# Splitting two weight loads by partition rows, and widening the row sums, in a grouped-query attention kernel

## The chip, the cores and the metric

The kernel runs on one core of a Trainium2 chip. The metric is device time in microseconds (us) of one execution; times quoted are medians. A ratio is the mean time of one kernel's fast runs over the mean of the other's fast runs in the same rounds on the same chip, so it is not quite the ratio of the quoted medians. "Fast" excludes runs more than 1.5% above the fastest of the same kernel.

## The reference

```python
# B=8, Sq=4, D=512, Hq=32, Hkv=8, Sk=2048, Dh=128, all bf16
q = (x @ wq).reshape(B, Sq, Hq, Dh).transpose(0, 2, 1, 3)
k = jnp.repeat(k_cache, 4, axis=1); v = jnp.repeat(v_cache, 4, axis=1)
scores = jnp.einsum("bhqd,bhkd->bhqk", q, k) * Dh ** -0.5
p = softmax(scores)
o = jnp.einsum("bhqk,bhkd->bhqd", p, v)
out = o.transpose(0, 2, 1, 3).reshape(B, Sq, Hq * Dh) @ wo
```

The K and the V cache are 33.6 MB each, wq and wo 4.2 MB each. Everything is read once, 75.5 MB in all, and little is written.

## The kernel before

All loads go out on one queue, from SyncE, in program order: x, wq, then K and V in blocks of 1 MiB (two heads of one batch, a "unit"; there are 32), then wo in blocks of 1 MiB and less. Every load but the small one of x (32 rows) covers 128 partitions. The code is shortened here and below.

```python
def load_wo(p, r0, n):
    rows = wo[p * HP * 128 : (p + 1) * HP * 128, :].rearrange("(q r) j -> q r j", r=WR)
    nc.sync.dma_start(wo_sb[:, p, r0 : r0 + n, :], rows[:, r0 : r0 + n, :])

nc.sync.dma_start(x_sb[:, :], x.flatten_outer_dims())
nc.sync.dma_start(wq_sb[:, :, :], wq.rearrange("(p r) n -> p r n", r=R))   # 128 rows of 32 KB
# ... K and V loads; after the last V load:
for w in range(G2 - 1):
    load_wo(w, 0, WR)            # three blocks: 128 rows of 8 KB
load_wo(G2 - 1, 0, 4); load_wo(G2 - 1, 4, 2); load_wo(G2 - 1, 6, 2)
```

The row sums of the softmax come from products with a matrix of ones, added up by VectorE (DVE):

```python
LC = 8
def norms(u):
    l_ps = psum_l.tile([128, LC, NQ], FP32, tag="l", name="l_ps")     # NQ = 32
    for c in range(0, C, LC):                                          # C = 32
        nc.tensor.matmul(l_ps[:, :, :], lhsT=ones[:, :], rhs=pr[:, c : c + LC, :],
                         start=(c == 0), stop=(c + LC == C))
    nc.vector.tensor_reduce(out=l_sb[:, :], in_=l_ps[:, :, :].rearrange("d c q -> d q c"),
                            axis=AX, op=ADD)
    nc.vector.reciprocal(r_sb[:, :], l_sb[:, :])

for step in range(-L - 1, NH):          # two steps (hf = 0, 1) to a unit
    # ... transposes of K and scores, some steps ahead
    if step >= 0:
        if hf == 1:
            norms(u)
        values(step)
```

The softmax here doesn't subtract the row's maximum and nothing guards it: scores larger than these inputs give would overflow.

Of the kernel before, what the change touches and what calls it, by code (L numbers as in the profile page):

```python
# [7 lines left out]

BF16 = mybir.dt.bfloat16
FP32 = mybir.dt.float32  # L10
EXP = mybir.ActivationFunctionType.Exp


@with_exitstack
def kernel(
# [9 lines left out]
    nc = tc.nc  # L25
# [7 lines left out]
    R = D // 128  # L33
# [12 lines left out]
    WR = HP  # L46
    DH = D // 2
    AX = mybir.AxisListType.X
    LC = 8
    ADD = mybir.AluOpType.add  # L50
    assert Dh == 128 and C == 32 and NQ == 32

# [14 lines left out]
    wq_sb = const.tile([128, R, HqDh], BF16, name="wq_sb")  # L67
# [3 lines left out]
    wo_sb = const.tile([128, G2, WR, D], BF16, name="wo_sb")  # L71
# [29 lines left out]

    def load_wo(p, r0, n):
        rows = wo[p * HP * 128 : (p + 1) * HP * 128, :].rearrange("(q r) j -> q r j", r=WR)
        nc.sync.dma_start(wo_sb[:, p, r0 : r0 + n, :], rows[:, r0 : r0 + n, :])

    nc.sync.dma_start(x_sb[:, :], x.flatten_outer_dims())
    nc.sync.dma_start(wq_sb[:, :, :], wq.rearrange("(p r) n -> p r n", r=R))
    loads = []
    for u in range(NU + KA):
        if u < NU:  # L110
# [27 lines left out]
    for p in range(G2):  # L138
        psq = psum_s.tile([128, HP, T], FP32, tag="s", name="psq")
        for h in range(HP):  # L140
# [30 lines left out]
    def scores(i):  # L171
        u, hf = divmod(i, 2)
        p, b = units[u]
        pr = probs[u % len(probs)]
        s_ps = psum_s.tile([128, HC, NQ], FP32, tag="s", name="s_ps")
        q2 = qT_all[:, p, b, :, :].rearrange("d h s -> d (h s)")
# [5 lines left out]
        for g in range(2):  # L182
            rows = slice(g * 64, (g + 1) * 64)
            cols = slice(g * NQ // 2, (g + 1) * NQ // 2)
            nc.scalar.activation(  # L185
                out=pr[rows, hf * HC : (hf + 1) * HC, cols], in_=s_ps[rows, :, cols], func=EXP
            )
# [3 lines left out]
    def values(i):  # L191
# [3 lines left out]
        if hf == 0:  # L195
            o_ps[u] = psum_o.tile([128, NQ], FP32, tag="o", name="o_ps")
        for c in range(HC):
# [11 lines left out]
    def norms(u):  # L209
        pr = probs[u % len(probs)]  # L210
        l_ps = psum_l.tile([128, LC, NQ], FP32, tag="l", name="l_ps")
        for c in range(0, C, LC):
            nc.tensor.matmul(  # L213
                l_ps[:, :, :],
                lhsT=ones[:, :],
                rhs=pr[:, c : c + LC, :],
                start=(c == 0),
                stop=(c + LC == C),
            )
        l_sb = small.tile([128, NQ], FP32, tag="l_sb", name="l_sb")  # L220
        nc.vector.tensor_reduce(  # L221
            out=l_sb[:, :], in_=l_ps[:, :, :].rearrange("d c q -> d q c"), axis=AX, op=ADD
        )
        r_sb = small.tile([128, NQ], FP32, tag="r_sb", name="r_sb")
        nc.vector.reciprocal(r_sb[:, :], l_sb[:, :])  # L225
# [38 lines left out]
    for step in range(-L - 1, NH):  # L264
        i, j = step + L + 1, step + L
        if i < NH:
            transpose_part(i, 0)
        if 0 <= j < NH:
            scores(j)
        if i < NH:  # L270
            transpose_part(i, 1)
        u, hf = divmod(step, 2)
        if step >= 0:
            p, b = units[u]
# [4 lines that stand above are left out]
                finish(u)  # L279
            elif p > 0 and b == 1:  # L280
                to_tokens(p - 1)
            elif p > 0 and b == 2:
                to_wo_rows(p - 1)
        load_ready(min((i + 1) // 2, NU), max((step + 1) // 2, 0))
        if step == NH - 1 - 2 * VB:
            assert not loads
            for w in range(G2 - 1):
                load_wo(w, 0, WR)
            load_wo(G2 - 1, 0, 4)
            load_wo(G2 - 1, 4, 2)  # L290
            load_wo(G2 - 1, 6, 2)
# [54 lines left out]
```

## Time and profile before

| | before |
|---|---|
| time, median (lowest to highest) | 195.31 us (194.30 to 196.41) |
| span in the profile | 193.6 us |
| mean rate of the loads | 393 GB/s |
| last V load lands | 178.23 us |
| last wo load lands | 188.17 us |
| last matrix product ends | 190.38 us |

The next line is from the page of the kernel before, the part in 40 equal slices of the span (4.84 us each): how much the DMA engines moved in each slice.

```profile
GB/s 223 433 386 423 421 423 415 425 418 413 420 415 420 416 420 418 421 416 418 418 420 418 418 420 423 416 416 416 416 421 416 421 420 418 415 420 418 321 107 7
```

Apart from the first slice and the last three, the rate is about 420 GB/s. Such a flat line suggests that the transfers set the pace and not an engine; the chain in the prediction agrees, most of it being waits for loads. The prediction below shows how the end of the kernel is read.

### The profile page before, as it was taken

The numbers are of one execution on the slowest core, as the hardware profiler recorded it, in microseconds if no ns is written. First come the engines' busy times: TensorE is split into PE (matmuls) and PEld (weight loads), VectorE is DVE, ScalarE is ACT, GpSimd is POOL, SyncE is SP. The second block draws the span as 40 slices with busy tenths as digits, with TensorE's granted clock in tenths as the row PEclk, the third lists the DMA queues.
The fourth block names the chain that finished last, engine by engine and source line by source line (L and its number), as shares of the span: only waits on it lengthen the run. The fifth ranks groups of instructions, "written<-read, shape, count | busy, mean of one in ns | idle before, by whom it ended". The sixth has DMA issues, their size and how long they took to land.

```text
span 193.6 us, 7489 instructions
## 1 busy us (share of the span) xinstructions
PE 147.5 (76%) x3428; PEld 135.4 (70%) x3428; DVE 99.0 (51%) x211; ACT 84.0 (43%) x166; POOL 0.7 (0%) x6
## 2 busy tenths in 40 slices
PE   1029768999888786977777799878787799785893
PEld 0029768888788776877777788777777788774441
DVE  6003454666656554655555576555555576544300
ACT  2003766555555554444555555424455555550000
POOL 1000000000000000000000000000000000000000
PEclk9999999999999999999999999999999999999699
DMA  6999999999999999999999999999999999999720
GB/s 223 433 386 423 421 423 415 425 418 413 420 415 420 416 420 418 421 416 418 418 420 418 418 420 423 416 416 416 416 421 416 421 420 418 415 420 418 321 107 7
DMA packets 10352, 76.05 MB, mean 393 GB/s; under 512 B 1168, under 2 KB 1232, under 8 KB 1616
## 3 DMA queue, kind: packets, MB, share of 16 engines
q1 hardware_dynamic: 10320, 75.57, 94.2%
q8 instruction: 27, 0.44, 0.9%
q14 instruction: 5, 0.04, 0.1%
HBM read 75.53 MB, written 0.03 MB: 390 GB/s over the span
## 4 chain that ended last, share of the span: by engine, by line
DMA 79%; PE 12%; ACT 3%; DVE 2%; issue 1%; SPq 0%; DVEq 0%
DMA k_sb<-in_k_cache_dram 63%; DMA v_sb<-in_v_cache_dram 10%; DMA wq_sb<-in_wq_dram 6%; PE out_ps L297 4%; ACT kt L166 2%; PE kp L163 2%; PE psq L143 2%; DVE kt L168 2%; PE s_ps L179 2%; ACT probs L185 1%; PE o_ps L199 1%; PE l_ps L213 1%; PE nat L242 1%; PE perm L257 0%; DVE l_sb L221 0%
## 5 line engine op out<-in xcount | busy, mean ns | idle before, releaser
L168 DVE COPY kt<-kp 128x1024 bf16<-128x1024 bf16 x96 | 65.6, 688 | 66.9 <-PE kp L163 66.2
L163 PE MATMUL kp<-ident,k_sb 128*128 128x128 bf16 x1024 | 77.0, 219 | 19.7 <-DMA k_sb<-in_k_cache_dram 19.5
L185 ACT ACTIVATE probs<-s_ps 64x256 bf16<-64x256 f32 x128 | 48.4, 378 | 74.1 <-PE s_ps L179 73.4
L163 PEld LDWEIGHTS <-k_sb 128*128 128x128 bf16 x1024 | 58.0, 97 | 23.2 <-DMA k_sb<-in_k_cache_dram 22.0
L179 PE MATMUL s_ps<-qT_all,kt 128*128 128x32 bf16 x1024 | 37.9, 176 | 6.7 <-ACT kt L166 5.1
L179 PEld LDWEIGHTS <-kt 128*128 128x128 bf16 x1024 | 33.1, 96 | 7.5 <-ACT kt L166 6.0
L199 PE MATMUL o_ps<-probs,v_sb 128*128 128x32 bf16 x1024 | 35.7, 176 | 2.7 <-DMA v_sb<-in_v_cache_dram 2.3
L199 PEld LDWEIGHTS <-v_sb 128*128 128x128 bf16 x1024 | 33.4, 96 | 3.9 <-DMA v_sb<-in_v_cache_dram 3.2
L166 ACT COPY kt<-kp 128x1024 bf16<-128x1024 bf16 x32 | 32.4, 1012 | 0.8
L213 PE MATMUL l_ps<-probs,ones 128*128 128x256 bf16 x128 | 19.2, 272 | 0.0
L221 DVE TENSOR_REDUCE l_sb<-l_ps 128x32 f32<-128x256 f32 x32 | 13.3, 416 | 5.2 <-PE l_ps L213 5.2
L225 DVE RECIPROCAL r_sb<-l_sb 128x32 f32<-128x32 f32 x32 | 11.3, 353 | 1.1
L213 PEld LDWEIGHTS <-ones 128*128 128x128 bf16 x128 | 11.0, 98 | 1.0 <-issue 0.2
L143 PE MATMUL psq<-xT_sb,wq_sb 128*128 128x32 bf16 x128 | 3.6, 187 | 9.3 <-DMA wq_sb<-in_wq_dram 9.3
L143 PEld LDWEIGHTS <-wq_sb 128*128 128x128 bf16 x128 | 3.5, 104 | 9.5 <-DMA wq_sb<-in_wq_dram 9.5
L297 PE MATMUL out_ps<-wo_sb,oP 128*32 128x512 bf16 x32 | 8.5, 427 | 0.0
L314 ACT CAST out_sb<-out_ps 32x256 bf16<-32x256 f32 x1 | 0.4, 362 | 17.8 <-DVE out_sb L313 17.8
L230 DVE TENSOR_TENSOR oT_all<-o_ps,r_sb 128x32 bf16<-128x32 f32 x32 | 6.1, 192 | 3.3
L150 ACT ACTIVATE qT_all<-psq 128x256 bf16<-128x256 f32 x4 | 1.5, 385 | 13.8 <-PE psq L143 13.8
L297 PEld LDWEIGHTS <-oP 128*32 128x32 bf16 x32 | 3.4, 109 | 4.3 <-issue 1.7
L248 DVE COPY nat_sb<-nat 32x1024 bf16<-32x1024 bf16 x4 | 2.7, 678 | 3.8 <-PE nat L242 3.8
L262 DVE COPY oP<-perm 128x256 bf16<-128x256 bf16 x4 | 1.2, 292 | 5.1 <-PE perm L257 5.1
(17 smaller groups left out, 16.4 us busy)
## 6 DMA issues: line engine op xcount, KB each, us to landing
k_sb<-in_k_cache_dram SPq DMA_DIRECT2D x32, 1024.0 KB, 19.9
v_sb<-in_v_cache_dram SPq DMA_DIRECT2D x32, 1024.0 KB, 19.9
wq_sb<-in_wq_dram SPq DMA_DIRECT2D x1, 4096.0 KB, 12.2
wo_sb<-in_wo_dram SPq DMA_DIRECT2D x3, 1024.0 KB, 21.3
wo_sb<-in_wo_dram SPq DMA_DIRECT2D x1, 512.0 KB, 20.0
wo_sb<-in_wo_dram SPq DMA_DIRECT2D x2, 256.0 KB, 16.5
x_sb<-in_x_dram SPq DMA_DIRECT2D x1, 32.0 KB, 1.6
out_dram<-out_sb SPq DMA_DIRECT2D x1, 32.0 KB, 1.5
```

The costliest lines, as they stand in the source:

```text
L143: nc.tensor.matmul(psq[:, h, :], lhsT=wq_sb[:, r, hh * 128 : (hh + 1) * 128], rhs=xT_sb[:, r, :], start=(r == 0), stop=(r == R - 1),)
L163: nc.tensor.transpose(kp[:, c, :], ks[u][:, c0 + c, :], ident[:, :])
L166: nc.scalar.copy(out=k_t[:, :, :], in_=kp[:, :, :])
L168: nc.vector.tensor_copy(out=k_t[:, :, :], in_=kp[:, :, :])
L179: nc.tensor.matmul(s_ps[:, c, :], lhsT=k_t[:, c % (HC // 2), :], rhs=q2, start=True, stop=True)
L185: nc.scalar.activation(out=pr[rows, hf * HC : (hf + 1) * HC, cols], in_=s_ps[rows, :, cols], func=EXP)
L199: nc.tensor.matmul(o_ps[u][:, :], lhsT=vs[u][:, cc, :], rhs=pr[:, cc, :], start=(cc == 0), stop=(cc == C - 1),)
L213: nc.tensor.matmul(l_ps[:, :, :], lhsT=ones[:, :], rhs=pr[:, c : c + LC, :], start=(c == 0), stop=(c + LC == C),)
L221: nc.vector.tensor_reduce(out=l_sb[:, :], in_=l_ps[:, :, :].rearrange("d c q -> d q c"), axis=AX, op=ADD)
L225: nc.vector.reciprocal(r_sb[:, :], l_sb[:, :])
L230: nc.vector.tensor_tensor(out=oT_all[:, p * HP : (p + 1) * HP, b, :], in0=o_ps[u][:, :].rearrange("d (h s) -> d h s", h=HP), in1=r_sbs[u][ ...
L297: nc.tensor.matmul(out_ps[:, :], lhsT=oP[p][:, r, :], rhs=wo_sb[:, p, r, :], start=(p == 0 and r == 0), stop=(p == G2 - 1 and r == WR - 1),)
```

## The change

The loads of 128 rows are cut by partition. As the prediction works out, the DMA engines fall into an early and a late group of eight. The change, as the prediction reads it, gives eight engines more rows and the others fewer. The trace doesn't number the engines; "the first eight" are here those that loads of 8 rows use. Moreover each pair of 512-wide products replaces four 256-wide ones, which leaves out 128 PE instructions in all.

```diff
+PARTS = [(0, 112), (112, 120), (120, 128)]
@@
-    LC = 8
+    LC = 16
@@ def load_wo(p, r0, n):
-        nc.sync.dma_start(wo_sb[:, p, r0 : r0 + n, :], rows[:, r0 : r0 + n, :])
+        for lo, hi in PARTS if n == WR else [(0, 128)]:
+            nc.sync.dma_start(wo_sb[lo:hi, p, r0 : r0 + n, :], rows[lo:hi, r0 : r0 + n, :])
@@
-    nc.sync.dma_start(wq_sb[:, :, :], wq.rearrange("(p r) n -> p r n", r=R))
+    for lo, hi in PARTS:
+        nc.sync.dma_start(wq_sb[lo:hi, :, :], wq.rearrange("(p r) n -> p r n", r=R)[lo:hi])
```

## The prediction

The sum of rival B came to 204.3 us. It holds two terms, 7.3 us for the two small wq loads and 5.6 us for the six of wo: they took a packet of an 8-row load to last four times as long (4 x 1.213 = 4.85 us at wq). The factor was assumed. Two milder cases of B came to 200 and 195 us.

> **What bounds the kernel now.** I read the page's utilisation strip first, then the chain of work that ended last (its shares, then in order of time), then the DMA issues, the queue table and the groups. The strip and the queue table:
>
> ```profile
> DMA  6999999999999999999999999999999999999720
> q1 hardware_dynamic: 10320, 75.57, 94.2%
> q8 instruction: 27, 0.44, 0.9%
> ```
>
> The 16 DMA engines are 90% busy or more in slices 2 to 37; 75.57 MB are moved in 193.6 us. Only the last three slices fall off, and not at once (7, 2, 0). That ramp is what the change aims at. The second queue brings instructions: 27 packets, 0.44 MB, so 16 KB each. The chain, in order of time, shows the end:
>
> ```profile
> 1.17 12.16 DMA wq_sb<-in_wq_dram
> ...
> 159.30 18.93 DMA v_sb<-in_v_cache_dram
> 178.23 0.05 issue
> 178.28 0.56 PE o_ps L199 x16
> 178.84 0.46 PE l_ps L213 x4
> 179.30 0.02 issue
> 179.32 0.43 DVE l_sb L221
> ...
> 180.48 1.03 PE nat L242 x8
> 181.52 2.96 PE out_ps L297 x8
> 184.48 0.60 PE perm L257 x8
> 185.09 5.30 PE out_ps L297 x24
> 190.38 0.02 issue
> ```
>
> The end is set by the last V load, landing at 178.23, then 12.15 us of PE and DVE work to 190.38, then 3.2 us of eviction and output store. The last wo load only just stays off this path. A load lands when all 16 increments of its semaphore have come, and the trace holds the time of each. For the last V load they come at 171.63 plus 0.00, 0.13, 0.25, 0.25, 0.29, 0.96, 1.55, 2.44 us, and then 4.68, 4.83, 4.84, 4.93, 4.98, 5.04, 5.12, 6.60 us: **eight DMA engines are early and eight late**, by 0.7 against 5.1 us on average, though all have the same bytes. For the last wo load the eighth comes at 184.04, the ninth at 186.25, the last at 188.17. For the first K load all sixteen lie within 0.41 us, so the gap grows during the run.
>
> Its cause shows in the packet records. The 27 instruction packets start at 19.4, 25.9, 32.4 us and so on, one about every 6.2 us, and take 1.02 to 1.15 us where they meet data. Next to each, one 8 KB data packet takes 0.76 to 0.86 us instead of 0.31, and the lengths recur with every eighth fetch: 0.787 us at 20.4, 70.9, 121.8 and 172.0. So fetches go round eight engines, and each holds one back by about 1.5 us (the largest lag rises 0.41, 1.9, 3.4, 5.1, 6.6 us). Three to four fetches for each of eight engines are the 5 us.
>
> [...]27 packets of 16 KB for 6,858 PE instructions in the build[...]. [...]8 KB packets are almost all 309 to 321 ns long, with no mutual disturbance. [...]in the 32-row x load most 1 KB packets take 44 to 46 ns, but one of 71 and one of 60 overlap, together 85 ns, about two in turn.
>
> **The change part by part.**
> *Rows.* The first eight engines get 9 rows of wq instead of 8, the others 7; the same for three wo blocks. A 32 KB wq packet takes 1.213 us, an 8 KB one 0.31. So the first eight gain 1.21 + 3 x 0.31 = 2.14 us of work, and the last eight lose as much: just half of the 4.4 us gap, clearly the intent. If nothing else happens and the first eight are the early ones, the last V comes at 178.23 - 1.2 = 177.0 (late engines; the early ones, 174.07 + 1.2 = 175.3, are not in the way), and the last wo at about 186.1.
> wq itself is complete 1.2 us later. That delays the compute that catches up from 13.4 to 34.4 us, but queued loads cover it: each landing takes about 20 us from its issue, eight in flight.
> *Row sums.* Four 256-wide matmuls become two 512-wide. Per column PE streams alike: in the chain four take 0.46 us, and 24 matmuls of 512 take 5.30, thus 0.22 each and two 0.44. PE gains nothing on the path.
>
> ```profile
> L221 DVE TENSOR_REDUCE l_sb<-l_ps 128x32 f32<-128x256 f32 x32 | 13.3, 416 | 5.2 <-PE l_ps L213 5.2
> L213 PE MATMUL l_ps<-probs,ones 128*128 128x256 bf16 x128 | 19.2, 272 | 0.0
> L230 DVE TENSOR_TENSOR oT_all<-o_ps,r_sb 128x32 bf16<-128x32 f32 x32 | 6.1, 192 | 3.3
> ```
>
> The reduce reads 512 elements, not 256. Between 32 elements (192 ns, L230) and 256 (416 ns) the slope is 1.0 ns per element, so I estimate 416 + 256 = 672 ns. DVE grows by 32 x 0.256 = 8.2 us to 107, 55% of the span: hidden, except in the tail, where it adds 0.26 us. The builds differ by 128 PE instructions (6,858 to 6,730), half a fetch, worth under 1.5 us on one engine; I count zero.
> Sum if the balance works: -1.2 + 0.26 = **-0.95 us**, 194.3.
>
> **The rivals.**
> A. *The balance works*, as just summed: 194.3. For it: the amounts fit the measured gap exactly. Even then it can't reach 2%: the PE tail of 12.15 us follows V, and only the wq half of the gain comes before V.
> B. *The small loads collide[...].* [...] On the first eight engines the extra is then 2.14 + 7.3 + 5.6 = 15.0 us by the last wo: 184.04 + 15.0 = 199.1, plus two matmuls (0.45) and 3.2 us, plus the 1.6 us by which the measured time exceeds the span: 204.3. If blocks of seven rows collide as well[...], a queue calculation with these durations adds some 4 us: 208.[...] For B: [...]the overlapping pair; against it, most x packets, and that the row counts look chosen by someone who measured.
> C. *The first eight are the late ones.* V lands 1.2 us later, wo at 190.3, and the wo load becomes the end: 190.3 + 0.45 + 3.2 + 1.6 = 195.6; same.[...]
>
> **Range and chances.** I give B in a form that costs over 2% 0.53, and A, C or a mild B 0.45. A leaves a narrow cluster at 194 to 195.6, B a wide one from 199 to 208. The one number is the median of both, **200.0 us**, at B's lower edge; the range is 193.3 to 208.0. Faster by over 2% gets 0.02, since no sum comes near 191.3.
>
> **What would show it.** A: wq packets stay at 1.21 us, the sixteen increments of the last V span 4 us or less, V lands near 177, wo near 186, and the chain is the same with a reduce of about 0.67 us. B: wq packets of the 8-row loads take 3 to 5 us, those of wo up to 1.2, wq lands past 20 us, the DMA strip shows holes near slices 3 to 5, the chain ends in a wo load, and the early group of engines has become the late one. C: the spread at the last V grows to about 9 us. Packets of unchanged length beside a time over 199 would show that I have the wrong cause; so would a DVE or PE group that the chain goes through in the middle.

## The result, and the profile after

The changed kernel takes 219.06 us (218.23 to 221.55) against 195.31: ratio 1.12, 95% interval 1.111 to 1.129. It is slower by some 23 us, and outside the predicted range, on the side of rival B.

From its page: the DMA strip, the rates in its 40 slices (5.44 us each) and the two queues.

```profile
DMA  7999799999999999999999999999999999999730
GB/s 193 247 259 110 84 352 418 420 421 418 417 418 417 414 421 420 420 417 418 418 418 417 423 418 420 415 417 417 423 417 418 420 415 417 242 220 214 226 98 9
q1 hardware_dynamic: 10384, 75.57, 94.3%
q8 instruction: 26, 0.43, 0.8%
```

The two lines must be read together. The strip says that the engines are as busy as ever, 90% or more in nearly all slices. The rates say that while they were "busy" they moved 247 and 259 GB/s in slices 2 and 3, 110 and 84 in slices 4 and 5 (the strip has a 7 for slice 5), and 214 to 242 in slices 35 to 38. Between, in the loads of K and V that the change didn't touch, the rate is the old 420. So the loss lies in exactly two stretches: while wq is loaded, and from the first split wo block on. The strip counted slow packets as busy all the same: slice 4 has a 9 at 110 GB/s, as the later slices have at 420.

The chain of work that ended last, in order of time (start, duration, what; all in us):

```profile
2.06 27.02 DMA wq_sb<-in_wq_dram
29.08 0.02 issue
29.09 19.59 DMA k_sb<-in_k_cache_dram
...
174.62 0.33 SPq L99
174.95 0.05 issue
175.00 26.86 DMA wo_sb<-in_wo_dram
201.86 0.02 issue
201.87 8.86 DMA wo_sb<-in_wo_dram
210.73 0.14 issue
210.87 3.63 PE out_ps L301 x16
```

Before, the chain opened with 12.16 us of wq; now it has 27.02 us, and it ends in split wo loads instead of the last V load and a PE tail. Worked out from the loads' semaphore records, latest increment of each:

| lands at (us) | before | after | later by |
|---|---|---|---|
| wq: 112 rows / first 8 / second 8 | 13.33 (one load) | 21.17 / 24.88 / 29.08 | 15.8 |
| first K load | 15.83 | 31.32 | 15.5 |
| last K load | 166.84 | 182.18 | 15.3 |
| last V load | 178.23 | 198.28 | 20.1 |
| last wo load | 188.17 | 213.27 | 25.1 |

The 15.5 us lost at wq are still there at the last K load. Nothing makes them up, because from there on the transfers run at the same 420 GB/s as before. The other 9.8 us are lost at wo; some of that already hits the last V load, during which wo was under way: the first wo load's earliest increment comes at 188.90 us, the last V load's latest at 198.28.

How long the packets took, again from the records (medians; the 112 rows in groups of 16 by order of start):

```
wq, 32 KB packets        before 1.21 us    after: first 112 rows 1.6 to 2.3 us, the 16 of the 8-row loads 4.88 us
K beside the 8-row loads before 0.31 us    after: 1.24 us (8 KB packets, between 16 and 24 us)
wo, 8 KB packets         before 0.31 us    after: 0.59 us (between 186 and 192 us)
```

The row sums, from the groups of the changed kernel (busy us, mean ns, then idle before):

```profile
L225 DVE TENSOR_REDUCE l_sb<-l_ps 128x32 f32<-128x512 f32 x32 | 21.8, 682 | 9.3 <-PE l_ps L217 9.3
L217 PE MATMUL l_ps<-probs,ones 128*128 128x512 bf16 x64 | 19.9, 393 | 0.0
```

The wide reduce takes 682 ns, where 672 were predicted, and PE gains nothing (19.9 us busy where it had 19.2).

### The profile page after: what moved, and what is told of

It reads as the page before. It is cut to its first block, busy times and chain, and to the rows that moved or that the text cites. A ratio compares the mean times of both kernels' runs of the same rounds, so it can differ in the third digit from the quotient of the medians.

```text
span 217.7 us, 7373 instructions
## 1 busy us (share of the span) xinstructions
PE 150.8 (69%) x3364; PEld 130.6 (60%) x3364; DVE 107.5 (49%) x211; ACT 84.0 (39%) x166; POOL 0.7 (0%) x6
## 4 chain that ended last, share of the span: by engine, by line
DMA 95%; PE 3%; SPq 1%; issue 0%; DVE 0%; ACT 0%
DMA k_sb<-in_k_cache_dram 66%; DMA wo_sb<-in_wo_dram 16%; DMA wq_sb<-in_wq_dram 12%; PE out_ps L301 2%; PE kp L167 0%; SPq L111 0%; PE l_ps L217 0%; DVE out_sb L317 0%; PE o_ps L203 0%; SPq L109 0%; PE s_ps L183 0%; ACT out_sb L318 0%; SPq L99 0%; SPq L89 0%
## 5 line engine op out<-in xcount | busy, mean ns | idle before, releaser
L167 PE MATMUL kp<-ident,k_sb 128*128 128x128 bf16 x1024 | 78.0, 220 | 17.8 <-DMA k_sb<-in_k_cache_dram 17.2
L167 PEld LDWEIGHTS <-k_sb 128*128 128x128 bf16 x1024 | 59.1, 98 | 20.4 <-DMA k_sb<-in_k_cache_dram 19.3
L203 PEld LDWEIGHTS <-v_sb 128*128 128x128 bf16 x1024 | 34.1, 97 | 16.9 <-DMA v_sb<-in_v_cache_dram 6.8
L203 PE MATMUL o_ps<-probs,v_sb 128*128 128x32 bf16 x1024 | 36.3, 177 | 8.1 <-DMA v_sb<-in_v_cache_dram 6.6
L225 DVE TENSOR_REDUCE l_sb<-l_ps 128x32 f32<-128x512 f32 x32 | 21.8, 682 | 9.3 <-PE l_ps L217 9.3
L217 PE MATMUL l_ps<-probs,ones 128*128 128x512 bf16 x64 | 19.9, 393 | 0.0
L301 PE MATMUL out_ps<-wo_sb,oP 128*32 128x512 bf16 x32 | 9.8, 467 | 1.9 <-DMA wo_sb<-in_wo_dram 1.9
L217 PEld LDWEIGHTS <-ones 128*128 128x128 bf16 x64 | 4.9, 98 | 0.0
```

The costliest lines, as they stand in the source:

```text
L167: nc.tensor.transpose(kp[:, c, :], ks[u][:, c0 + c, :], ident[:, :])
L203: nc.tensor.matmul(o_ps[u][:, :], lhsT=vs[u][:, cc, :], rhs=pr[:, cc, :], start=(cc == 0), stop=(cc == C - 1),)
L301: nc.tensor.matmul(out_ps[:, :], lhsT=oP[p][:, r, :], rhs=wo_sb[:, p, r, :], start=(p == 0 and r == 0), stop=(p == G2 - 1 and r == WR - 1),)
```

## The experiments

All runs gave correct results. The first four take the change apart and look for the late engines; the rest ask what makes the split loads slow. The theory in the expectations is that a packet's length depends on which partitions the engines write at the same time.

**rowsums.** Edit: only `LC = 16`.

> Only the row sums are changed (two 512-wide products instead of four 256-wide); all loads as before. Theory[...]: this part is worth little, 195 to 196 us, reduce at 0.68 us each, last V load landing near 178 us. Rival (the wide row sums hold PE or DVE back and cost several us): 198 us or more.

Measured: 196.16 us against 195.20, ratio 1.0056 (1.0009 to 1.0104). Its chain at the end, which answers to that of the kernel before:

```profile
178.36 0.56 PE o_ps L199 x16
178.92 0.46 PE l_ps L213 x2
179.40 0.70 DVE l_sb L221
```

The V load lands as before, and the reduce on this path takes 0.70 us where it took 0.43. This part alone costs something like half a per cent, 1.1 us, of which the longer reduce explains 0.27; it isn't where 23 us went.

**wqonly.** Edit: only the wq load goes through `PARTS`.

> Only wq is split into 112 + 8 + 8 rows. Theory: wq is complete near 29 us as in the changed kernel, the first K load lands 15.5 us later than before, the delay is never recovered, time 208 to 211 us. Rival (the wq delay is hidden by queued loads and the loss lies at the wo loads): under 199 us.

Measured: 211.09 us, ratio 1.0822 (1.075 to 1.090), that is +16.0 us. In the profiled run (209.25 us) wq is complete at 28.23 us, and the rates show the same hole at the start and none at the end:

```profile
GB/s 203 235 281 133 90 320 418 420 418 420 415 417 423 417 415 422 414 420 422 417 422 418 414 422 423 415 420 420 412 420 423 417 417 420 422 414 422 364 100 6
```

**woonly.** Edit: only the three wo blocks go through `PARTS`.

> Only three wo blocks are split. Theory: wo packets stretch as in the changed kernel, 8 to 10 us are lost at the end, 203 to 206 us; with the wq part the two losses add up to the 24 us of the changed kernel. Rival (wo is hidden behind the PE tail): 196 us.

Measured: 204.63 us, ratio 1.051 (1.045 to 1.057), +10.0 us. The last wo load lands at 198.15 us in the profile, 10.0 us later than before, and the hole is at the end only:

```profile
GB/s 213 420 414 423 425 419 419 422 417 419 417 410 420 422 415 420 420 419 414 425 419 414 423 417 417 423 410 417 425 419 417 417 419 396 213 220 228 208 122 6
```

The three parts alone sum to 16.0 + 10.0 + 1.1 = 27.1 us, where the whole change costs 0.12 x 195.3 = 23.4. For the row sums the reason can be read: in the changed kernel the chain ends in a wo load, so the slower reduce isn't on it. The rest of the difference (2.6 us) I have not tested; the wq loss alone varied between its own runs (209.25 to 212.25). In the profiled runs alone it is gone: their spans are 13.2 (wq), 9.2 (wo) and 1.0 us (row sums) longer than the 193.6 of before, together 23.4, and that of the whole change is 24.1 longer.

**probe.** Which engines are the late ones? Edit: sixteen tiny marker loads of 1, 2, ... 16 rows ahead of V loads.

```diff
+        if 12 <= u < 28:
+            k = u - 11
+            nc.sync.dma_start(mark[u - 12][:k, :], wq[:k, :32])
```

> The kernel before with 16 tiny marker loads of 1 to 16 rows of 64 bytes, one ahead of each V load of units 12 to 27. [...]Theory of the change's author (the first eight are the early engines): the marker of 8 rows shows only early times, the late ones appear with 9 rows and up. Rival (late engines are spread over both halves): the marker of 8 rows shows early and late times. Time within 1 per cent of before.

Measured: 196.17 us in one look. A marker of k rows (up to 15) gave one increment about half a microsecond after its issue, and then, near the times of the load before it, k more. The author took a marker of k rows to use k engines, those of the marker before and one more, the k-th. The count fits the increments (k of them, and in the changed kernel eight to each load of 8 rows); the order is an assumption. The k times then show where the first k engines stand behind the load before. Around the marker of 8 rows:

```
K load before it, 16 increments:  117.19 117.21 117.32 117.39 117.48 117.49 118.11 118.58 | 120.28 120.42 120.46 120.48 120.49 120.62 120.67 120.83
marker of 8 rows:                 117.41 117.52 117.61 117.68 118.30 118.78 | 120.68 120.71
```

Six of the first eight engines are early and **two are late**. By that order the series tells which: the markers of 1 to 5 rows show only early times, those of 6 and 7 rows add a late one each, and the eighth engine is early. So, in that order, the late engines are the sixth and seventh, and six of the last eight. The idea that the first eight engines are the early ones was not right. That the late engines are those that fetch is read from the trace before: the spread of a load's increments jumps from 0.41 to 1.90, 1.97 to 3.44, 3.58 to 5.07 and 5.14 to 6.58 us at the loads that land just after the fetches at 19.4, 69.9, 120.8 and 171.0 us, every eighth fetch. No run changed the fetches to test it.

**halves.** Edit: `PARTS = [(0, 64), (64, 128)]` for wq only: no odd count, no engine left out.

> wq as two loads of 64 rows (partitions 0-63, then 64-127), each on 16 engines with 4 rows each. No count is odd and no engine is left out. [...]packets take about 2.4 us instead of 1.21, wq is complete near 23 us, time about 205. Rival (112 is slow as a count that is no power of two, or the loss is that of eight engines): wq at 13 to 14 us, time 195 to 196.

Measured: 205.89 us, ratio 1.0508 (1.044 to 1.058). All packets but the first round (which was longer before too: the first 16 packets of wq took 1.27 to 2.17 us, the others 1.21 to 1.27) take 2.37 to 2.57 us. From 2 to 24 us the mean busy share of the 16 engines was 0.98 at 209 GB/s, so none was left out. wq is complete at 24.04 us, and the rates of the first slices are about half:

```profile
GB/s 148 205 238 199 238 422 417 422 413 427 414 422 411 421 413 424 421 416 419 417 421 419 422 413 424 414 424 416 416 416 417 424 419 417 419 417 416 354 123 6
```

**middle.** Edit: `PARTS = [(32, 96), (0, 32), (96, 128)]` for wq only. The first load has as many rows as each half above, 64, but another base, in the source too, since rows and partitions go together here.

> wq as three loads on 16 engines: first partitions 32-95 (64 rows, 4 to an engine), then 0-31 and 96-127 (32 rows each, 2 to an engine). Same count as in the run with halves, only the base is moved[...]: the 64 packets of the first load take 1.21 us (after the first round[...]), those of the other two 2.56 us; wq complete near 18.5 us, time 200 to 201. Rival (64-row loads are slow as such): all packets 2.56 us, time near 206.

Measured: 201.76 us, ratio 1.030 (1.023 to 1.037). The 64 packets of the first load take 1.21 to 1.25 us after the first round, and it lands at 9.47 us; a load of the same 64-row size from partition 0 landed at 14.03. From 2 to 9 us the engines' mean busy share was 1.08 (sums of overlapping packets can pass 1) at 375 GB/s, from 9 to 19 us 0.89 at 199. The two loads of 32 rows have packets of 1.80 to 2.57 us, and wq is complete at 19.36, somewhat later than expected. The rates show the step from the good load to the bad ones within four slices (5.0 us each):

```profile
GB/s 209 340 222 242 422 417 415 424 420 417 417 414 417 420 420 419 417 419 422 417 420 419 417 422 419 417 420 417 417 419 415 419 420 422 414 422 411 289 65 7
```

The count of rows is not what matters: 64 rows gave packets of 1.21 to 1.25 us from partition 32 and of 2.37 to 2.57 us in the halves. Which partitions the engines write at the same time is the likely cause; the source rows moved along with them, which the next two runs rule out.

**adjacent** and **spread.** These put the 8-row loads to the test with the source rows held fixed. wq is loaded as before; behind it, the last 16 rows of wq are read once more into the wo tile, which is overwritten later.

```diff
+    spare = wo_sb[:, :, :, :].rearrange("d p r j -> d (p r j)")
+    wq_rows = wq.rearrange("(p r) n -> p (r n)", r=R)
+    nc.sync.dma_start(spare[112:120, :], wq_rows[112:120])      # spread: spare[0:32:4, :]
+    nc.sync.dma_start(spare[120:128, :], wq_rows[120:128])      # spread: spare[1:32:4, :]
```

> wq as before in one load of 128 rows; behind it two extra loads of 8 rows of 32 KB (the last 16 wq rows once more) into 8 neighbouring partitions of the wo tile, 112-119 and 120-127. The result is unchanged, since wo overwrites them. [...]the 16 extra packets take some 4.9 us each, and the first K load lands about 9 to 10 us later than before; time 203 to 206. Rival (what was slow is the block of 112 rows, or the reading of these rows): packets near 1.2 us, time about 197.

> The same two extra loads from the same rows, but into partitions 0,4,...,28 and 1,5,...,29[...]: packets of 1.2 us, the first K load 2.4 us later, time 196 to 198. Rival (a load on eight engines, or these source rows, is slow whatever the partitions): packets of 4.9 us and time as with neighbouring partitions.

Measured, adjacent: 204.66 us, ratio 1.0455 (1.039 to 1.052). The 16 extra packets have a median of 5.2 us, and the first K load lands at 27.07. Measured, spread: 196.50 us (one of the four runs was slow), ratio 1.0007 (0.991 to 1.010). Its extra packets take 1.21 to 1.22 us and the first K load lands at 18.16. The same stretch of both, 13.4 to 24 us from the start (its length, busy us and instructions of each engine, then the PE clock, the DMA engines' busy share and the rate); adjacent first:

```profile
13.40:24.00 10.60, 3.58 (x128) 3.48 (x128) 0.00 (x0) 1.54 (x4) 0.00 (x0) 0.89 0.81 80
```

```profile
13.40:24.00 10.60, 9.18 (x209) 8.98 (x210) 2.77 (x4) 3.58 (x8) 0.00 (x0) 1.00 1.00 419
```

80 against 419 GB/s, with the same loads queued from the same rows, differing in the destination partitions only. In the adjacent run the last eight engines, which should be through the first K load by 16 us (before, its latest increment came at 15.83), finish it at 24.0 to 24.9: their 8 KB packets take up to 1.59 us. That led to the next run.

**lowports.** Edit: as adjacent, into `spare[0:8, :]` and `spare[8:16, :]`. The question is whether only the packets into the crowded partitions are slow (the first case below) or those of other engines' loads too (the rival).

> As the run with neighbouring partitions, but the two extra 8-row loads go to partitions 0-7 and 8-15[...]: the extra packets still take 4.9 to 5.3 us, but the first K load comes at 15.4 to 16 us on the last eight engines, and their 8 KB packets stay at 0.31 us. Rival[...]: the K packets stretch to about 1.3 us as in that run, and the K load comes at 24 us on them. Time in both cases 201 to 206.

Measured: 202.60 us, ratio 1.0346 (1.026 to 1.043). The one profiled run was slow (205.29 us), so only its first 25 us are used, where the effect is severalfold. The extra packets of the second load take 4.18 to 4.20 us (those of the first, which start while wq is still loading, 2.96 to 4.15), less than the 4.9 to 5.3 expected; why is open. The 8 KB packets of K between 13 and 18 us have a median of 1.16 us. The stretch from 13 to 18 us ran at 128 GB/s, with the engines busy throughout (columns as above):

```profile
13.00:18.00 5.00, 2.83 (x106) 2.84 (x107) 0.00 (x0) 0.82 (x3) 0.00 (x0) 1.00 1.03 128
```

The last eight engines finish the first K load at 21.7 to 22.5 us. (The increments don't name engines; the other eight, at 24.2 to 24.8, are taken for those with the extra loads.) Without extra rows the first K load's increments came at 15.42 to 15.83 us; here even the earliest came at 21.7. The theory that only the packets into the crowded partitions are slow falls: **8-row loads into neighbouring partitions held up the K packets of the engines without extra rows too** (1.16 us instead of 0.31). The K load covers all 128 partitions; to which of them its slow packets went, and by what path they were held up, these runs don't show.

**five.** Edit: as spread, but `spare[0:20:4, :]` and `spare[1:20:4, :]`, so five engines only.

> As the spread run, but with five rows twice, partitions 0,4,..,16 and 1,5,..,17, so on the first five engines alone[...]. If the markers are right, the extra 2.4 us fall on early engines only: the last V load's latest increment stays at 178.0 to 178.5 us, as before, where the spread run had 179.0. Rival (the first eight are alike): 179.

Measured: 196.22 us in one look. The last V load is complete at 178.03 us, as before (178.23), although five engines had 2.4 us more to do; with eight engines it was 179.02. In the spread run two of the engines given extra work were late ones already, in agreement with the markers. The difference is small and each rests on one profile.

**earlynorms** and **wofirst.** A look for a kernel that beats both, in the PE tail. Edit of the first: `if hf == 0: norms(u)` in place of `hf == 1`. The second also loads the first wo block ahead of the last V block and multiplies it before the last unit.

> Kernel before with one move: the row sums of a batch are issued ahead of the first half of its value products, not ahead of the second half; they need no V. At the end, the 0.46 us of sums, the 0.43 us reduce and the 0.36 us reciprocal then lie before the last V lands. If the PE tail after the last V sets the end: 0.8 us less, 194.4 to 195, ratio near 0.996. If the last wo load sets it: no change.

> As the run before, and the first wo block is loaded ahead of the last V block with its eight products ahead of the last unit. The last V lands 2.5 us later (near 180.7), but 3 us of products go out of the tail. Expected: the same as the run before within 0.5 us, since the last wo load at 188.2 us then leaves little to gain (floor near 189 us for the last product). A gain over 1.5 us would show that the tail's order mattered more than its loads.

Measured: 195.16 us, ratio 0.9956 (0.991 to 1.001), and 195.43 us, ratio 0.9973 (0.993 to 1.002), both against 195.89. Neither is clear of no change at all. In the first one's profile (the fastest of its six runs) the last product ends at 189.2 us, 1.2 us earlier than before, with the last V load at 178.13; that fits the expected gain but does not prove it.

## Why the prediction was right or wrong

*What bounds the kernel, and rival B*: right. The small loads slow each other. The wq packets of the 8-row loads took 4.88 us, where B had 4.85; wq landed past 20 us; the loss has the two places named; the chain ends in a wo load. Spread against adjacent (packets of 1.21 to 1.22 us against 5.2) shows that the partitions written are the cause, not the number of engines or rows, and middle against halves (1.21 to 1.25 against 2.37 to 2.57) agrees; for wo's smaller packets this is carried over from wq, not tested. That 4.88 came so near to 4.85 is partly luck: the second extra load had 5.29 to 5.31 us in adjacent and 4.18 to 4.20 in lowports. One of B's signs failed: the DMA strip shows no holes but a single 7; the hole is in the GB/s line.

*The size of B*: wrong, and this is the step that failed: "**On the first eight engines the extra is then 2.14 + 7.3 + 5.6 = 15.0 us by the last wo: 184.04 + 15.0 = 199.1**". It assumes that the last eight engines go on undisturbed, so that the 4.4 us lead of the early engines cushions the loss, and that the block of 112 rows is nearly harmless ("some 4 us" in an afterthought). What the runs showed in its place:

- The block of 112 rows was the largest term. Without collisions seven rows would be in at 13.33 - 1.21 = 12.1 us; it took until 21.17, so 9.1 us more. In the wq-only profile it took until 19.39.
- The two 8-row loads of wq took from 21.17 to 29.08, 7.9 us, where B had 2 x 4.85 = 9.7. The term was right for an engine (4.88 to a packet), but the first of these packets started at 16.3, beside the end of the block of 112 rows.
- All 16 engines were held up, not eight. The earliest increment of the first K load came at 27.40 us instead of 15.42, so there was no undisturbed group and no lead to use up. The adjacent and lowports runs show the same with no block of 112 rows.
- wo cost 9.8 us, where B had 3 x 0.31 + 5.6 = 6.5.

So the last wo load came at 213.27, not 199.1. The 14.2 us between them add up: 6.8 at wq (15.3 still late at the last K load, where B had 1.2 + 7.3), 3.3 at wo, and 4.1 for the lead that the early engines were to use up (188.17 against 184.04). Even B's worst case, 208 (from a queue calculation), was far too mild. The single number of 200.0, the median of two outcomes, described neither.

*Rival A*: wrong twice. Its first condition, packets of unchanged length, failed. And even its aim would have been missed: "the first eight are the early ones" is not so, since two of them are late ones. I didn't know which engines are the late ones, and made of it an all-or-nothing rival C; by the markers the truth lay between.

*The row sums*: right in their parts. 682 ns for the predicted 672, nothing on PE, and in the tail +0.27 us (0.70 against 0.43). The rowsums run cost 1.1 us (interval 0.2 to 2.0, which takes in the 0.26 predicted). I counted nothing for half a fetch less; there are 26 instead of 27.

*Hiding the late wq*: the prediction said that queued loads cover a late wq. It was said of 1.2 us, which no run tested; what came was 15.8 us with the DMA engines themselves slow, which the queue did not cover: the K loads stood behind it in the same queue.

## What to carry to other kernels

Before you balance work over DMA engines, check which partitions they will write at the same time: here 8 rows of 32 KB into neighbouring partitions had packets of 5.2 us, into every fourth partition 1.21 to 1.22. The loads that moved rows between engines cost 23 us to mend a lag of 4.4, and they slowed the K packets beside them too (1.24 us instead of 0.31). Read the DMA busy share together with the GB/s line; here slices that were 90% busy at a quarter of the usual rate were the mark of the collision. And before giving work to "the idle engines", find out by a marker load which ones they are.
